# First weights' conversions pinned to the program's order, their low parts on GpSimd, and half of the first batch's sums over v on GpSimd

## The chip, the core and the metric

One core of a Trainium2 chip runs the whole program in one launch. The metric is the device time of an execution in microseconds (us); lower is better. Five engines run side by side, each through its own queue in order: TensorE (PE, its weight loads PEld), VectorE (DVE), ScalarE (ACT), GpSimd (POOL) and SyncE (SP, which here issues every DMA).

## What is computed

Attention with keys and values pooled by 8 along the sequence, for 8 batches of 8 heads, 576 positions and 64 columns a head; then two feed-forward blocks on the 4608 tokens. Cut to what matters:

```
k_p = k.reshape(B, H, 72, 8, 64).mean(axis=3);  v_p likewise
scores = scale * q @ k_p.T;  attn = softmax(scores)
x = (attn @ v_p) as 4608 tokens x 512
h = x @ w_in;  x = maximum(0.01 * h, h) @ w_out          # 512 x 2048, 2048 x 512
xn = x / rms(x) * rms_g
out = (silu(xn @ w_gate) * (xn @ w_val)) @ w_out2
```

## The kernel before

Every fp32 operand of the large products is held as two fp32r tensors, a rounded high part and a low part that is the difference (`split`, line 90: the high part is a cast on ScalarE, L92, the low part a subtraction, L95, on the engine that the caller names). A product then takes three matmuls, high by high, high by low and low by high.

The tokens go through the first feed-forward in nine tiles of 512 (`j` 0 to 8). For each of 16 blocks `f` of 128 hidden columns, `h_unit` (L592) multiplies by the w_in block and makes the two halves of the activation (`ghl`: ScalarE L98 twice, then a VectorE subtraction L605), and `y_unit` (L628), two blocks later, multiplies by the w_out block. In tile 0 the first eight blocks are done for tokens 0 to 255 first, and again for tokens 256 to 511 at the end of the tile (`h0_0_256` and on), because only the first two q tiles of batch 0 are through attention when the tile begins.

The 32 weight blocks (w_i0, w_o0, w_i1, ... w_o15) are read from memory as raw pieces and converted on chip by the class `Weights`, once. A piece is 128 x 512; the last four blocks come as eight pieces of 128 x 256. One piece takes four steps:

- a first pass in place over the upper words on ScalarE (a `prelu`, listed under L98) and one over the lower words on VectorE (TENSOR_SCALAR, L141),
- a join of the two on VectorE (SCALAR_TENSOR_TENSOR, L149),
- the cast to the high part on ScalarE (L92), and
- the subtraction for the low part (L95), on GpSimd and VectorE by turns: w_in blocks on GpSimd and w_out blocks on VectorE; of the halves of a block the first on GpSimd and the second on VectorE.

`step()` ends one piece (join, cast, low part), loads what may be loaded, and begins the next one (the two first passes). Raw pieces lie in slots that later weights take over, the eight half pieces in a ring of three (`raw`) that k and v of the following batches use too.

Attention of batch 0 comes first: `k_prep` and `v_prep` sum eight rows (for batch 0 a VectorE reduction, L239 and L254; for later batches GpSimd adds in halves, `pool_sum`, L229, then L245 or L259), `v_prep` spreads the sum over two heads (`vm`, GpSimd L263, one buffer) and splits it (`vb`). `step_s` is the softmax of one q tile (VectorE L331, L332, L337 to L340 around ScalarE's exponential, L336), `step_x` transposes it and splits it (`at`), `step_av` multiplies by v and leaves the first feed-forward's input (`xhl`).

The order of each engine's queue comes from a scheduler that places an instruction as soon as its own model of time has its operands ready; a conversion whose piece has come in may so stand ahead of attention that was written before it. `keep_in_program_order` pins an instruction behind the one that the program wrote before it on the same engine. From the second half on the order is the written one.

Of the kernel before, what the change touches and what calls it, by code (L numbers as in the profile page):

```python
# [8 lines left out]
F32 = mybir.dt.float32  # L9
# [7 lines left out]
HI, LO = 0, 1  # L17
# [5 lines left out]
def pooled_attention_then_two_ffns(  # L23
# [13 lines left out]
    nc = tc.nc  # L37
# [59 lines left out]
    def prelu(out, in_, alpha, scale=1.0):  # L97
        return nc.scalar.activation(out=out, in_=in_, func=AF.Prelu, scale=scale, alpha=alpha)  # L98
# [8 lines left out]
    class Weights:  # L107
# [5 lines left out]
        def __init__(self, todo, ahead):  # L113
            self.todo = todo
            self.ahead = ahead
            self.loaded = []
            self.begun = []
            self.done = {}
            self.n = 0

        def left(self):
            return bool(self.todo or self.loaded or self.begun)
# [10 lines left out]
        def begin(self):  # L133
            x = self.loaded.pop(0)
            t = x[2]
            top, low = t[:, :, 1], t[:, :, 0]


            prelu(top.bitcast(F32), top.bitcast(F32), 2.0 ** 32, scale=2.0 ** -112)

            nc.vector.tensor_scalar(  # L141
                out=low, in0=low.bitcast(U32), scalar1=0.9374 * 2.0 ** -29, scalar2=None, op0=ALU.mult
            )
            self.begun.append(x)

        def end(self):
            key, at, t, mk = self.begun.pop(0)
            top, low = t[:, :, 1], t[:, :, 0]
            nc.vector.scalar_tensor_tensor(  # L149
                out=top, in0=top, scalar=3, in1=low, op0=ALU.logical_shift_left, op1=ALU.bitwise_or  # L150
            )
            if key not in self.done:
                self.done[key] = mk(f"w_{key[0]}{key[1]}")
            w = self.done[key]
            self.n += 1
            lo_eng = nc.gpsimd if self.n % 2 else nc.vector
            split(nc.scalar, w[:, HI, at], lo_eng, w[:, LO, at], top.bitcast(F32))

        def step(self):
            if self.begun:  # L160
# [87 lines left out]
    def v_prep(b, r):  # L248
        rest = r >= NP
        n = R3 if rest else P  # L250
        x = vraw.pop((b, r))[0:n]
        vs = ap.tile([P, D], F32, tag="vs", bufs=2, name=f"vs{b}_{r}")[0:n]
        if b == 0:
            nc.vector.tensor_reduce(  # L254
                out=vs, in_=x.rearrange("p (r d) -> p d r", r=POOL), axis=AX.X, op=ALU.add
            )
        else:
            pool_sum(x)
            nc.gpsimd.tensor_tensor(out=vs, in0=x[:, 0:D], in1=x[:, D:2 * D], op=ALU.add)  # L259
        m = mask_rest.rearrange("p q h -> p (q h)") if rest else mask_main  # L260
        c = m.shape[1]
        vm = ap.tile([P, 4, D], F32, tag="vm", bufs=1, name=f"vm{b}_{r}")[0:n, 0:c]
        nc.gpsimd.tensor_tensor(  # L263
            out=vm, in0=vs.unsqueeze(1).to_broadcast([n, c, D]),
            in1=m.unsqueeze(2).to_broadcast([n, c, D]), op=ALU.mult,
        )
        if rest:

            t = ap.tile([R3, 4, D], F32R, tag="vbr", bufs=2, name=f"vb{b}_{r}")
            nc.scalar.activation(out=t, in_=vm, func=AF.Copy)  # L270
            z = slice(2 * R1, 3 * R1)
            nc.vector.tensor_tensor(out=t[z], in0=vm[z], in1=t[z].bitcast(F32), op=ALU.subtract)
        else:
            t = ap.tile([P, 2, 2, D], F32R, tag="vb", bufs=4, name=f"vb{b}_{r}")
            split(nc.scalar, t[:, HI], nc.vector, t[:, LO], vm)
        vb[b, r] = t
# [68 lines left out]
    at = {}  # L345
# [234 lines left out]
        W1.load()  # L580
    for x in before:
        run_step(x)
        if x[0] in "sx" and x[2] > 0:
            W1.step()

    gp = {}
# [669 lines left out]
```

## Time and profile before

| | us |
|---|---|
| median of 3 executions | 1825.57 (1824.18 to 1827.65) |
| the profiled execution | 1826.16 |
| its span, first to last instruction | 1824.4 |
| TensorE busy in the span | 1764.8 (97%) |
| VectorE busy | 881.1 (48%) |
| ScalarE busy | 669.4 (37%) |
| GpSimd busy | 557.0 (31%) |

The span is 1.8 us shorter than the execution's time. The shares are means over stages that differ much, so the rows further down are taken by stretch. Start times are counted from the first instruction. In a timeline row the bracket holds the engine's idle time before the instruction and what ended it; neighbours on an engine overlap by some hundredths to a few tenths of a microsecond, so durations add up to somewhat more than the time from start to start. GpSimd's own durations are rough.

### The profile page before, as it was taken

The numbers are of one execution on the slowest core, as the hardware profiler recorded it, in microseconds if no ns is written. First come the engines' busy times: TensorE is split into PE (matmuls) and PEld (weight loads), VectorE is DVE, ScalarE is ACT, GpSimd is POOL, SyncE is SP. The second block draws the span as 40 slices with busy tenths as digits, with TensorE's granted clock in tenths as the row PEclk, the third lists the DMA queues.
The fourth block names the chain that finished last, engine by engine and source line by source line (L and its number), as shares of the span: only waits on it lengthen the run. The fifth ranks groups of instructions, "written<-read, shape, count | busy, mean of one in ns | idle before, by whom it ended". The sixth has DMA issues, their size and how long they took to land.

```text
span 1824.4 us, 23632 instructions
## 1 busy us (share of the span) xinstructions
PE 1764.8 (97%) x8596; PEld 1504.5 (82%) x8596; DVE 881.1 (48%) x1593; ACT 669.4 (37%) x1424; POOL 557.0 (31%) x691
## 2 busy tenths in 40 slices
PE   4899999999999999999999999999999999999999
PEld 3789887888888887888888878989787888988887
DVE  8974445463356555554244336344534533463331
ACT  5754334343343444343433332233232223322220
POOL 2653204243124252111211442244144114513330
PEclk9999999999999999999999999999999999999999
DMA  8832105446365445445442657687676567776562
GB/s 266 292 118 85 47 21 159 151 150 222 104 192 161 157 147 161 144 143 165 159 150 82 230 175 247 188 294 245 237 248 207 187 221 281 247 264 201 197 208 104
DMA packets 175556, 330.81 MB, mean 181 GB/s; under 512 B 54352, under 2 KB 90192, under 8 KB 174928
## 3 DMA queue, kind: packets, MB, share of 16 engines
q1 hardware_dynamic: 175440, 329.31, 54.9%
q8 instruction: 68, 1.11, 0.3%
q14 instruction: 48, 0.39, 0.1%
HBM read 277.87 MB, written 51.38 MB: 180 GB/s over the span
## 4 chain that ended last, share of the span: by engine, by line
PE 87%; DVE 4%; DMA 4%; POOL 2%; issue 1%; ACT 1%; SPq 1%; ACTq 0%; DVEq 0%; POOLq 0%
PE h L592 20%; PE y L628 20%; PE o L1089 14%; PE yv L1014 6%; PE yg L1014 6%; PE xv L1014 4%; PE wv L1014 4%; PE wg L1014 4%; PE xg L1014 4%; PE sc L325 2%; DMA wo<-wo 1%; PE av L395 1%; DMA xst<-y 1%; PE xt L369 1%; PE qt L303 1%
## 5 line engine op out<-in xcount | busy, mean ns | idle before, releaser
L592 PE MATMUL h<-xhl,w_i 128*128 128x512 f32 (+1 forms) x1824 | 438.6, 386 | 3.0 <-ACT xhl L92 1.5
L592 PEld LDWEIGHTS h<-xhl,w_i 128*128 128x128 f32 x1824 | 330.3, 191 | 67.7 <-DVE xhl L95 3.2
L1089 PE MATMUL o<-wo,u 128*128 128x512 f32 x1296 | 315.7, 391 | 5.1 <-DMA wo<-wo 5.1
L1089 PEld LDWEIGHTS o<-wo,u 128*128 128x128 f32 x1296 | 243.0, 188 | 54.1 <-issue 4.3
L628 PE MATMUL y<-ghl,w_o 128*128 128x512 f32 (+1 forms) x1296 | 285.1, 365 | 1.4 <-DVE ghl L605 1.4
L628 PEld LDWEIGHTS y<-ghl,w_o 128*128 128x128 f32 x1296 | 219.0, 191 | 35.1 <-DVE ghl L605 1.8
L605 DVE TENSOR_TENSOR ghl<-g,ghl 128x512 fp32r<-128x512 f32 (+1 forms) x152 | 114.5, 754 | 245.1 <-ACT g L98 241.9
L98 ACT ACTIVATE ghl<-h 128x512 fp32r<-128x512 f32 (+1 forms) x152 | 86.9, 572 | 227.6 <-PE h L592 227.1
L628 PE MATMUL y<-ghl,wr 128*128 128x512 f32 x624 | 158.6, 395 | 0.0
L628 PEld LDWEIGHTS y<-ghl,wr 128*128 128x128 f32 x624 | 115.1, 188 | 22.4
L95 POOL TENSOR_TENSOR u<-e2g,u 128x512 fp32r<-128x512 f32 (+1 forms) x25 | 29.6, 1182 | 287.1 <-ACT u L92 277.7
L229 POOL TENSOR_TENSOR v<-v 128x256 f32<-128x256 f32 (+2 forms) x84 | 61.3, 733 | 111.1 <-DMA v<-in_v_dram 108.5
L1014 PE MATMUL xv<-xa,av 128*128 128x512 f32 (+1 forms) x360 | 85.8, 374 | 6.1 <-ACT e1v L1042 6.1
L98 ACT ACTIVATE g<-h 128x512 f32<-128x512 f32 (+1 forms) x152 | 86.7, 571 | 0.0
L1014 PE MATMUL yv<-T,av 128*128 128x512 f32 (+1 forms) x360 | 85.3, 373 | 0.0
L1014 PE MATMUL yg<-T,ag 128*128 128x512 f32 (+1 forms) x360 | 83.9, 368 | 0.0
L1014 PE MATMUL xg<-xa,ag 128*128 128x512 f32 (+1 forms) x360 | 83.8, 368 | 0.0
L1014 PEld LDWEIGHTS xv<-xa,av 128*128 128x128 f32 x360 | 67.5, 192 | 16.2 <-ACT e1v L1042 6.7
L1014 PEld LDWEIGHTS yv<-T,av 128*128 128x128 f32 x360 | 67.8, 192 | 9.5
L1014 PEld LDWEIGHTS xg<-xa,ag 128*128 128x128 f32 x360 | 66.2, 188 | 9.5
L1014 PEld LDWEIGHTS yg<-T,ag 128*128 128x128 f32 x360 | 66.2, 188 | 9.4
L735 POOL TENSOR_TENSOR parts_g<-raw_g,parts_g 128x256 fp32r<-128x256 f32 (+1 forms) x48 | 33.6, 723 | 100.1 <-ACT parts_g L731 100.1
(166 smaller groups left out, 2594.8 us busy)
## 6 DMA issues: line engine op xcount, KB each, us to landing
wo<-wo SPq DMA_DIRECT2D x120, 512.0 KB
av<-op_v SPq DMA_DIRECT2D x90, 512.0 KB
ag<-op_g SPq DMA_DIRECT2D x90, 512.0 KB
wr<-wo SPq DMA_DIRECT2D x52, 512.0 KB
y<-ye SPq DMA_DIRECT2D x36, 256.0 KB
op_g<-parts_g SPq DMA_DIRECT2D x36, 256.0 KB
op_v<-parts_v SPq DMA_DIRECT2D x36, 256.0 KB
out_dram<-oe SPq DMA_DIRECT2D x36, 256.0 KB
```

Of the source, the lines that this page charges most:

```text
L95: lo_eng.tensor_tensor(out=lo, in0=src, in1=hi.bitcast(F32), op=ALU.subtract)
L98: return nc.scalar.activation(out=out, in_=in_, func=AF.Prelu, scale=scale, alpha=alpha)
L229: nc.gpsimd.tensor_tensor(out=x[:, :n], in0=x[:, :n], in1=x[:, n:2 * n], op=ALU.add)
L303: nc.tensor.transpose(pt[:, c * P:(c + 1) * P], x[:, c * P:(c + 1) * P], ident)
L325: nc.tensor.matmul(pt[:, i * n:(i + 1) * n], y[:, p, :], kblk[b % 2][:, p * n:(p + 1) * n], start=True, stop=True,)
L369: nc.tensor.transpose(pt[:, c * P:(c + 1) * P], e[:, c, 0:P], ident)
L592: nc.tensor.matmul(pt, w[:, sp, c * P:(c + 1) * P], x[:, mp, c, :], start=c == 0 and i == 0, stop=c == n_k - 1 and i == 2,)
L605: nc.vector.tensor_tensor(out=t[:, LO, :], in0=g, in1=t[:, HI, :].bitcast(F32), op=ALU.subtract)
L628: nc.tensor.matmul(pt, w[:, sp, m * P:(m + 1) * P], g[:, mp, a - c0:a - c0 + n], start=ydone[j, a] == 1 and i == 0 and m % per_bank == 0, ...
L735: own(nc.gpsimd.tensor_tensor(out=d[:, :, LO, :], in0=x, in1=d[:, :, HI, :].bitcast(F32), op=ALU.subtract))
L1014: nc.tensor.matmul(pt, wt[:, a, c, sp, :], xt[:, mp, :], start=start and c == 0 and i == 0, stop=c == 1 and i == 2, skip_group_check=not s ...
L1089: nc.tensor.matmul(pt, u[:, sp, m * P:(m + 1) * P], w[:, mp, :], start=f == 0 and i == 0, stop=f == F2 - 1 and i == 2,)
```

## The change

Three edits. The two first passes of every piece are pinned behind what the program wrote ahead of them on their engines, and `step()` is now also called after the second q tile's softmax, after both `step_x` of the first two tiles and after each of the four `av0`, so that it runs seven times and not twice before tile 0 begins. The low parts of all weights are GpSimd's. Of the first batch's six sums over v, numbers 0, 2 and 4 are made by GpSimd as for the later batches.

```diff
--- before.py
+++ after.py
@@ -116,7 +116,6 @@
             self.loaded = []
             self.begun = []
             self.done = {}
-            self.n = 0
 
         def left(self):
             return bool(self.todo or self.loaded or self.begun)
@@ -136,11 +135,14 @@
             top, low = t[:, :, 1], t[:, :, 0]
 
 
-            prelu(top.bitcast(F32), top.bitcast(F32), 2.0 ** 32, scale=2.0 ** -112)
-
-            nc.vector.tensor_scalar(
+            x1 = prelu(top.bitcast(F32), top.bitcast(F32), 2.0 ** 32, scale=2.0 ** -112)
+
+            x2 = nc.vector.tensor_scalar(
                 out=low, in0=low.bitcast(U32), scalar1=0.9374 * 2.0 ** -29, scalar2=None, op0=ALU.mult
             )
+
+            tc.keep_in_program_order(x1)
+            tc.keep_in_program_order(x2)
             self.begun.append(x)
 
         def end(self):
@@ -152,9 +154,7 @@
             if key not in self.done:
                 self.done[key] = mk(f"w_{key[0]}{key[1]}")
             w = self.done[key]
-            self.n += 1
-            lo_eng = nc.gpsimd if self.n % 2 else nc.vector
-            split(nc.scalar, w[:, HI, at], lo_eng, w[:, LO, at], top.bitcast(F32))
+            split(nc.scalar, w[:, HI, at], nc.gpsimd, w[:, LO, at], top.bitcast(F32))
 
         def step(self):
             if self.begun:
@@ -250,7 +250,7 @@
         n = R3 if rest else P
         x = vraw.pop((b, r))[0:n]
         vs = ap.tile([P, D], F32, tag="vs", bufs=2, name=f"vs{b}_{r}")[0:n]
-        if b == 0:
+        if b == 0 and r % 2:
             nc.vector.tensor_reduce(
                 out=vs, in_=x.rearrange("p (r d) -> p d r", r=POOL), axis=AX.X, op=ALU.add
             )
@@ -580,7 +580,7 @@
         W1.load()
     for x in before:
         run_step(x)
-        if x[0] in "sx" and x[2] > 0:
+        if x[0] in ("x", "av0") or x[0] == "s" and x[2] > 0:
             W1.step()
 
     gp = {}
```

The lines move a little: L141 and L149 of before are L140 and L151 of after. The new order at three places follows. First VectorE's queue in the first batch's softmax (ex0_0 and ex0_1 are the exponentials of the first two q tiles, st their maxima and sums, raw_i0 to raw_o1 raw weight pieces, vs sums over v). Before:

```order
L332 TENSOR_TENSOR ex0_1_212<-sc0_1_0_214,st0_1_213 128x288
L337 TENSOR_REDUCE st0_0_196<-ex0_0_195 128x8
L141 TENSOR_SCALAR raw_o0_0_121<-raw_o0_0_121 128x512
L95 TENSOR_TENSOR vb0_2_249<-vm0_2_247,vb0_2_249 128x128
L332 TENSOR_TENSOR ex0_1_212<-sc0_1_1_219,st0_1_213 128x288
L338 TENSOR_SCALAR st0_0_196<-st0_0_196 128x8
L149 SCALAR_TENSOR_TENSOR raw_o0_0_121<-raw_o0_0_121 128x512
L339 RECIPROCAL st0_0_196<-st0_0_196 128x8
L254 TENSOR_REDUCE vs0_5_266<-first12_123 96x64
L141 TENSOR_SCALAR raw_i1_0_128<-raw_i1_0_128 128x512
L337 TENSOR_REDUCE st0_1_213<-ex0_1_212 128x8
L340 TENSOR_TENSOR ex0_0_195<-ex0_0_195,st0_0_196 128x576
```

After:

```order
L332 TENSOR_TENSOR ex0_1_212<-sc0_1_1_219,st0_1_213 128x288
L339 RECIPROCAL st0_0_196<-st0_0_196 128x8
L340 TENSOR_TENSOR ex0_0_195<-ex0_0_195,st0_0_196 128x576
L337 TENSOR_REDUCE st0_1_213<-ex0_1_212 128x8
L95 TENSOR_TENSOR vb0_2_253<-vm0_2_251,vb0_2_253 128x128
L338 TENSOR_SCALAR st0_1_213<-st0_1_213 128x8
L339 RECIPROCAL st0_1_213<-st0_1_213 128x8
L340 TENSOR_TENSOR ex0_1_212<-ex0_1_212,st0_1_213 128x576
L140 TENSOR_SCALAR raw_i0_0_119<-raw_i0_0_119 128x512
L254 TENSOR_REDUCE vs0_5_272<-first12_123 96x64
L95 TENSOR_TENSOR at0_0_279<-xt0_0_284,at0_0_279 128x4x128
L95 TENSOR_TENSOR vb0_3_260<-vm0_3_258,vb0_3_260 128x128
```

The first passes and joins of the first pieces have left the softmax: the first one now follows the second tile's last softmax step, L340.

Second, GpSimd's queue where the weights begin (w_i0, w_o0, ... low parts; vm the spread sums of v; k1 the keys of batch 1). Before:

```order
L263 TENSOR_TENSOR vm0_4_261<-vs0_4_259,mask_rest_65 96x256
L95 TENSOR_TENSOR w_i1_408<-raw_i1_0_128,w_i1_408 128x512
L263 TENSOR_TENSOR vm0_5_268<-vs0_5_266,mask_rest_65 96x256
L95 TENSOR_TENSOR w_i2_466<-raw_i2_0_139,w_i2_466 128x512
L95 TENSOR_TENSOR w_i3_534<-raw_i3_0_143,w_i3_534 128x512
L95 TENSOR_TENSOR w_i9_946<-raw_i9_0_809,w_i9_946 128x512
L229 TENSOR_TENSOR k1_0_872<-k1_0_872 128x256
L95 TENSOR_TENSOR w_i4_610<-raw_i4_0_309,w_i4_610 128x512
L229 TENSOR_TENSOR k1_1_879<-k1_1_879 128x256
L229 TENSOR_TENSOR k1_0_872<-k1_0_872 128x128
L229 TENSOR_TENSOR k1_2_904<-k1_2_904 128x256
```

After:

```order
L263 TENSOR_TENSOR vm0_4_267<-vs0_4_263,mask_rest_65 96x256
L263 TENSOR_TENSOR vm0_5_274<-vs0_5_272,mask_rest_65 96x256
L95 TENSOR_TENSOR w_i0_297<-raw_i0_0_119,w_i0_297 128x512
L95 TENSOR_TENSOR w_o0_320<-raw_o0_0_121,w_o0_320 128x512
L95 TENSOR_TENSOR w_i1_336<-raw_i1_0_128,w_i1_336 128x512
L95 TENSOR_TENSOR w_o1_351<-raw_o1_0_130,w_o1_351 128x512
L95 TENSOR_TENSOR w_i2_366<-raw_i2_0_139,w_i2_366 128x512
L95 TENSOR_TENSOR w_o2_379<-raw_o2_0_141,w_o2_379 128x512
L95 TENSOR_TENSOR w_i3_442<-raw_i3_0_143,w_i3_442 128x512
L229 TENSOR_TENSOR k1_0_918<-k1_0_918 128x256
L229 TENSOR_TENSOR k1_1_925<-k1_1_925 128x256
L229 TENSOR_TENSOR k1_0_918<-k1_0_918 128x128
```

Seven low parts now stand in a row ahead of batch 1's keys, the w_out blocks among them, and none before the last vm.

Third, ScalarE's queue while the first av are made (L98 on a raw piece is its first pass, L92 on a w its cast, xhl the input of the first feed-forward). Before:

```order
L98 ACTIVATE raw_i3_0_143<-raw_i3_0_143 128x512
L376 ACTIVATE atr0_0_274<-xr0_1_300 96x2x128
L92 ACTIVATE w_i2_466<-raw_i2_0_139 128x512
L92 ACTIVATE w_o2_528<-raw_o2_0_141 128x512
L98 ACTIVATE raw_o3_0_145<-raw_o3_0_145 128x512
L98 ACTIVATE raw_i6_0_613<-raw_i6_0_613 128x512
L92 ACTIVATE xhl0_318<-av0_0_0_313 128x256
L92 ACTIVATE w_i3_534<-raw_i3_0_143 128x512
L98 ACTIVATE raw_o6_0_666<-raw_o6_0_666 128x512
L92 ACTIVATE xhl0_318<-av0_0_1_321 128x256
```

After:

```order
L92 ACTIVATE w_o0_320<-raw_o0_0_121 128x512
L98 ACTIVATE raw_i1_0_128<-raw_i1_0_128 128x512
L92 ACTIVATE xhl0_332<-av0_0_0_327 128x256
L92 ACTIVATE w_i1_336<-raw_i1_0_128 128x512
L98 ACTIVATE raw_o1_0_130<-raw_o1_0_130 128x512
L92 ACTIVATE xhl0_332<-av0_0_1_343 128x256
L92 ACTIVATE xhl0_332<-av0_0_2_358 128x256
L92 ACTIVATE w_o1_351<-raw_o1_0_130 128x512
L98 ACTIVATE raw_i2_0_139<-raw_i2_0_139 128x512
L92 ACTIVATE w_i2_366<-raw_i2_0_139 128x512
L98 ACTIVATE raw_o2_0_141<-raw_o2_0_141 128x512
```

A piece's first pass now comes after the cast of the piece before it, where first passes ran ahead by up to five pieces.

SyncE's queue keeps its 797 rows; from the fifth block's loads on, those of weights, k, v and q change places by a few rows.

## Rows read from the trace of the kernel before

**Rows 1.** Page, part 2: busy tenths of TensorE in 40 equal slices.

```profile
PE   4899999999999999999999999999999999999999
```

**Rows 2.** Busy time by stretch; clock, DMA share and GB/s in the last columns.

```profile
0.00:37.20 37.20, 11.95 (x41) 8.49 (x41) 29.78 (x55) 19.26 (x50) 8.93 (x25) 1.00 0.84 257
45.00:113.00 68.00, 61.59 (x419) 55.85 (x419) 67.29 (x126) 49.29 (x121) 42.39 (x52) 0.97 0.68 231
120.00:130.00 10.00, 9.04 (x41) 8.31 (x42) 7.58 (x18) 6.53 (x16) 2.92 (x6) 0.66 0.49 153
140.00:400.00 260.00, 256.24 (x1371) 220.24 (x1370) 122.92 (x272) 99.16 (x254) 73.73 (x134) 0.99 0.34 102
```

The columns are the stretch, its length, then busy time (instructions) of PE, PEld, DVE, ACT and POOL, the granted clock, the DMA share and GB/s.

**Rows 3.** Timeline of TensorE: start, duration, instruction, count, idle before and releaser.

```profile
37.22 1.01 PE L395 MATMUL av<-at,vb 128*128 128x256 f32 x3 [2.50 <-DVE at L95]
...
120.96 1.01 PE L395 MATMUL av<-at,vb 128*128 128x256 f32 x3 [2.58 <-DVE at L95]
...
129.35 0.51 PE L395 MATMUL av<-at,vb 128*128 128x256 f32 x3
...
134.54 0.66 PE L325 MATMUL sc<-kblk,qT 128*128 128x144 f32 x4
...
138.60 0.60 PE L303 MATMUL qt<-ident,q 128*128 128x128 f32 x4
...
140.00 1.68 PE L592 MATMUL h<-xhl,w_i 128*128 128x256 f32 x12
```

**Rows 4.** Timeline of VectorE in the first batch's attention.

```profile
12.70 0.45 DVE L331 TENSOR_REDUCE st<-sc 128x4 f32<-128x288 f32 x1
...
14.07 1.01 DVE L254 TENSOR_REDUCE vs<-first 128x64 f32<-128x512 f32 x1
...
17.52 0.43 DVE L141 TENSOR_SCALAR raw_i<-raw_i 128x512 int32<-128x512 uint32 x1 [1.87 <-DMA raw_i<-in_moe_w_in_dram]
...
36.48 0.69 DVE L95 TENSOR_TENSOR at<-xt,at 128x512 fp32r<-128x512 f32 x1
```

**Rows 5.** Timeline from 45 to 50 us, GpSimd first, then VectorE.

```profile
46.27 1.31 POOL L95 TENSOR_TENSOR w_i<-raw_i,w_i 128x512 fp32r<-128x512 f32 x1 [4.90 <-ACT w_i L92]
...
48.92 1.52 POOL L95 TENSOR_TENSOR w_i<-raw_i,w_i 128x512 fp32r<-128x512 f32 x1 [0.21 <-ACT w_i L92]
...
45.31 0.42 DVE L141 TENSOR_SCALAR raw_i<-raw_i 128x512 int32<-128x512 uint32 x1
45.65 0.68 DVE L149 SCALAR_TENSOR_TENSOR raw_o<-raw_o 128x512 int32<-128x512 int32 x1
...
46.59 1.53 DVE L149 SCALAR_TENSOR_TENSOR raw_i<-raw_i 128x512 int32<-128x512 int32 x1
...
49.42 1.31 DVE L605 TENSOR_TENSOR ghl<-g,ghl 128x256 fp32r<-128x256 f32 x1 [0.15 <-ACT g L98]
```

**Rows 6.** Timeline, single instructions of VectorE and GpSimd.

```profile
61.00 0.41 DVE L605 TENSOR_TENSOR ghl<-g,ghl 128x256 fp32r<-128x256 f32 x1
...
124.22 0.74 POOL L95 TENSOR_TENSOR w_i<-raw_i,w_i 128x256 fp32r<-128x256 f32 x1 [2.90 <-ACT w_i L92]
...
63.62 0.74 POOL L229 TENSOR_TENSOR k<-k 128x256 f32<-128x256 f32 x1 [0.77 <-DMA k<-in_k_dram]
...
55.47 0.45 POOL L229 TENSOR_TENSOR k<-k 128x128 f32<-128x128 f32 x1
...
57.15 0.31 POOL L245 TENSOR_TENSOR kp<-k 128x64 f32<-128x64 f32 x1
```

**Rows 7.** Groups by line and form, 45.0 to 112.9 us: busy, mean ns, idle before.

```profile
L149 DVE SCALAR_TENSOR_TENSOR raw_o<-raw_o 128x512 int32<-128x512 int32 x9 | 8.5, 947 | 0.1
L95 DVE TENSOR_TENSOR w_o<-raw_o,w_o 128x512 fp32r<-128x512 f32 x10 | 7.7, 771 | 0.0
...
L95 POOL TENSOR_TENSOR w_i<-raw_i,w_i 128x512 fp32r<-128x512 f32 x10 | 13.9, 1394 | 23.5 <-ACT w_i L92 23.5
```

**Rows 8.** Timeline of VectorE, one wait for a raw half piece.

```profile
118.59 0.84 DVE L141 TENSOR_SCALAR raw_o<-raw_o 128x256 int32<-128x256 uint32 x1 [4.96 <-POOL v L229]
```

## The prediction, made before the changed kernel was run

> **What bounds the kernel now.** I read the slices of the page first. TensorE is busy in nine tenths or more of every slice but the first, which holds 46 us [rows 1]; from 140 to 400 us it is busy for 256.24 of 260 us at a granted clock of 0.99 [rows 2]. Work that is moved among the other engines can therefore gain only ahead of 140 us, and what is gained there is carried to the end if the order after it is the same, as it is from the second half on and nearly so from tile 2. Next come the stretches. Until 37.2 us TensorE works for 11.95 us and VectorE for 29.78 [rows 2]: the program begins with a chain over VectorE. The first product with v starts at 37.22, released by VectorE's `at`, which ended at 37.17 [rows 3, 4]. From 45 to 113 us VectorE is busy for 67.29 of 68 us and GpSimd for 42.39 [rows 2].
>
> That last pair is not what it seems. A join takes 0.68 us at 45.65, and 1.53 at 46.59, where it ends half a microsecond behind the low part that GpSimd began at 46.27. A subtraction that takes 0.41 at 61.00 takes 1.31 at 49.42 beside the low part of 48.92 [rows 5, 6]. So VectorE's busy time there holds waits for GpSimd, and a low part costs VectorE nearly as much as if it ran there.
>
> The Trainium skill, page "SBUF — State Buffer", section "Who interferes with whom", says the same more sharply: an instruction of VectorE with two SBUF inputs, or in a two-port mode, and one of GpSimd that reads SBUF shut each other out for their whole length, and a reduction on VectorE does not take part. It speaks against this change twice, since subtractions go where they hold the shared port longer, and three reductions that leave it alone become adds that hold it. The rows at 46.59 and 49.42 agree. Without the lock VectorE would be freed by what it gives away (the rival with the whole head start, below); with it, the sum of the next paragraphs holds.
>
> **A check of that account.** Say that in-place passes, joins, low parts, `ghl` and `ex` products on VectorE and everything on GpSimd take one shared turn. From 45.0 to 112.9 us VectorE has 18 joins and 10 low parts at 0.68, 16 first passes at 0.42, 8 `ghl` at 0.41 and 4 at 0.68, and some 8.6 us of smaller ones: 40.4 us. GpSimd has 10 low parts at 1.31 and 2 halves at 0.74, batch 1's keys (5 times 0.74 + 0.45 + 2 x 0.31, so 9.1), and 9.7 of v (1.9 a sum, with 0.4 for vm): 33.4 [rows 5 to 7]. Together 73.8 us of durations in 67.9 us; neighbours overlap a little, which gives 1.08 us of durations for each us of time. The turn is full throughout. A change that adds to the turn loses there what it adds, divided by 1.08.
>
> **Part 1, the softmax ahead of the conversions.** Ahead of the second tile's `at` (36.48, rows 4) VectorE loses three sums (3 x 1.02), five first passes (2.1), five joins (3.4), two low parts (1.4) and one vb part (0.4), so 10.4 us, and the wait of 1.87 for the first raw piece, which by then will have come [rows 4, 5]. That alone would put `at` at 24.2. But the softmax can't begin before the first scores at 12.70 [rows 4], 13.5 us of VectorE's work stand between, which gives 26.2, and the six vm through one buffer go back and forth between three engines. I take 28 (bounds 26 and 30): a head start of 9.2 us for the first product.
>
> **Part 2, half of the sums on GpSimd.** Three times 0.74 + 0.45 + 0.31 = 4.5 us [rows 6]. GpSimd is busy for 8.93 of the first 37.2 us, so they are hidden; if the vm chain behind them were late it would cost up to those 4.5. I take nothing.
>
> **Part 3, the low parts.** Fourteen whole and four half ones leave VectorE (about 11.2 us) and cost GpSimd 14 x 1.31 + 4 x 0.74 = 21.3: 10.1 us more of the shared turn. And the pinned order puts each piece's first pass behind the cast of the piece before, so nothing is converted ahead.
>
> **The sum.** When the first low part starts, about 28 us, these are left for the turn. GpSimd: 28 x 1.31, 8 x 0.74, keys 9.1, five v of 1.9: 61.2. VectorE: 26 first passes, 27 joins, eight halves of each at six tenths, 8 `ghl` at 0.41 and 7 at 0.68, and 6.6 of small ones: 49.2. That is 110.4, over 1.08 102.2, and I add 1.5 for holes where a row of low parts has nothing beside it: the last piece is done at 131.7. The second half of w_i15 is two half pieces earlier (2 x 1.4 / 1.08 = 2.6), at 129.1. From there TensorE has 6 of the 12 matmuls of h_15 and 15 of y_13 before `h0_0_256`, 27 units of 256 columns at some 0.14 us (12 in 1.68) [rows 3], 3.6 us with overlap off: 132.7, where the kernel before has 140.00. But that one had by then done two av, two scores, a qt and a kt that the new order puts later (0.51 and 0.66 twice each and 0.60, rows 3: 2.9 by duration, of which I take 2.4 since neighbours overlap), and the second pair's `av` now waits for the last v of batch 1, behind the last low parts on GpSimd, for which I take 1.0. The gain is 140.0 - 132.7 - 2.4 - 1.0 = **3.9 us**.
>
> The head start of 9.2 us is thus mostly given back, since the stretch to the last conversion goes from TensorE's pace to that of the shared turn. What was late before also goes: at 118.59 VectorE had waited 4.96 us for a half piece with `at` queued behind it, and TensorE 2.58 for that `at` [rows 3, 8]; from 120 to 130 us the granted clock was 0.66, a mixture of 1.2 and 2.4 GHz behind that gap [rows 2]. This is in the 140.0.
>
> SyncE's queue: as many loads; those of the last half pieces wait for three buffers that v shares, and each waits for a low part on GpSimd, now the slowest engine of the chain. The stores of w_o0 to w_o7 in the same queue wait for GpSimd too. I take nothing for it, since the turn and not the loads was full before, and 4.96 us as the price of one late piece.
>
> The span would go from 1824.4 to 1820.5. The profiled execution was 1826.16, 0.6 above the median of 1825.57, so against the median I forecast 1821.7.
>
> **Rivals.**
>
> *The head start is kept whole.* If TensorE, not the turn, paces the new order (low parts of GpSimd falling beside VectorE work that reads PSUM: scores, maxima, `at`, `xhl`), 9.2 us stay: 1816.4. For it: 42.39 us of GpSimd in 68 leave room. Against: the turn was full in the same stretch.
>
> *No change.* The pinned steps overlap less than the free order did, 1.04 in place of 1.08: 106.2 us, the last piece at 135.7 with the holes, `h0_0_256` at 136.7, a gain of 140 - 136.7 - 3.4 = -0.1: 1825.7. For it: up to five first passes ran ahead before, none do now.
>
> *Slower: the chain through one piece.* Join (0.68), cast (about 0.7), low part (1.31) and the next join behind it: 2.7 us a piece, which uses the turn only part of the time, while keys, v and `ghl` come in lumps that hide little. Then durations pass one by one: 28 + 110.4 = 138.4, `h0_0_256` at 139.4, -2.8 us, and with one late half piece reaching TensorE as before (2.58 us) 5.4: 1831.0. The average step, counting a half as 0.6, may be 3.28 us before anything is lost; my sum has it at 3.16 and this case at 3.37. So a tenth of a microsecond a step decides.
>
> *The scheduler undoes it*, so that the new order is not the one meant: the rows of the order ahead rule that out, the softmax does come first.
>
> **How the numbers follow.** The forecast (a gain of 2 to 7 us) has 0.48, the whole head start 0.15, no change 0.20, slower 0.17. A measurement tells 0.2% from no change, 3.65 us. Of the forecast's 0.48, 0.33 lie beyond that; with the 0.15 of the head start faster has 0.48. Within 0.2% are 0.15 of the forecast, 0.20, and 0.01 of the slower case: 0.36. Slower has 0.16. The range leaves out the far end of the head start (0.06) and of the slower case (0.10): 1815.5 to 1829.5.
>
> **What would show it.** Right: the first av near 28 us; low parts on GpSimd in a row some 2.7 to 3.3 us apart; the last near 132; VectorE's joins and first passes often at 1.2 us or more; `h0_0_256` near 133. Wrong: first av after 31 (the vm chain), or the last low part before 126 (no full turn) or after 137 (the chain), or a clock below full over a long part of 60 to 130 us, since TensorE waiting for each low part could fall to the lower level; then its products would take twice as long, and that is in no term above.

## The result: ten microseconds slower, lost behind the conversions

| | before | after |
|---|---|---|
| median, us | 1825.57 | 1835.72 |
| lowest to highest | 1822.30 to 1831.46 | 1829.85 to 1840.99 |
| profiled execution | 1826.16 | 1840.99 |
| span of it | 1824.4 | 1839.3 |

The ratio is 1.0052, with a 95% interval of 1.0034 to 1.0070: slower by 6 to 13 us, outside the range of the prediction. The profiled execution of after is its slowest, so its trace shows more of the loss (14.9 us in the span) than the median (10.2).

The views of the profile of after in the order in which before was read. First the busy time by stretch (columns as in [rows 2]):

```profile
0.00:37.20 37.20, 16.83 (x62) 12.95 (x62) 26.84 (x49) 16.88 (x48) 14.00 (x34) 1.00 0.81 245
45.00:113.00 68.00, 59.97 (x371) 53.62 (x372) 62.59 (x105) 47.08 (x114) 50.77 (x54) 0.92 0.67 223
113.00:130.00 17.00, 17.00 (x118) 15.75 (x117) 11.12 (x22) 9.19 (x23) 8.44 (x11) 1.00 0.37 105
130.00:150.00 20.00, 13.36 (x88) 12.70 (x88) 7.83 (x16) 6.48 (x18) 12.78 (x25) 0.88 0.33 90
150.00:200.00 50.00, 46.04 (x314) 43.19 (x313) 27.73 (x58) 19.97 (x63) 20.91 (x42) 0.91 0.35 98
140.00:400.00 260.00, 249.59 (x1317) 214.49 (x1316) 123.74 (x266) 96.74 (x247) 77.95 (x147) 0.97 0.33 98
```

The same of before, for the stretches that [rows 2] lacks:

```profile
113.00:130.00 17.00, 14.42 (x76) 13.00 (x75) 9.51 (x21) 7.71 (x19) 5.51 (x10) 0.80 0.43 130
130.00:150.00 20.00, 20.00 (x159) 19.48 (x159) 10.31 (x20) 7.12 (x24) 13.14 (x26) 1.00 0.34 101
150.00:200.00 50.00, 49.98 (x330) 45.55 (x329) 24.41 (x55) 21.33 (x58) 20.02 (x38) 1.00 0.31 85
```

Until 37.2 us TensorE is busy for 4.9 us more than before. From 45 to 113 us it gives that back: 371 of its matmuls (of differing widths) fall in that stretch, 419 in before [rows 2]. From 113 to 130 it is ahead again, 17.00 us busy at full clock against 14.42 at 0.80. Then it turns. From 130 to 200 us it is idle for 10.6 us (70 less 13.36 and 46.04) where before had none, at a lower clock. The forecast had it that nothing behind 140 us would change.

TensorE's timeline shows the place (as in [rows 3]):

```profile
29.01 1.01 PE L395 MATMUL av<-at,vb 128*128 128x256 f32 x3 [1.40 <-DVE at L95]
...
125.59 0.87 PE L395 MATMUL av<-at,vb 128*128 128x256 f32 x6
...
133.13 0.51 PE L400 MATMUL av<-atr,vb 96*128 96x256 f32 x2 [2.78 <-DVE vb L272]
...
136.64 0.52 PE L592 MATMUL h<-xhl,w_i 128*128 128x256 f32 x3
...
145.79 0.80 PE L400 MATMUL av<-atr,vb 96*128 96x256 f32 x2 [3.86 <-DVE vb L272]
...
182.81 1.08 PE L369 MATMUL xt<-ident,ex 128*128 128x128 f32 x4 [3.42 <-DVE ex L340]
```

The first product with v came at 29.01, as forecast, and `h0_0_256` at 136.64. But the `av` of batch 1 now stop in the middle: `L400` multiplies by `vb1_4` and `vb1_5`, the last two v pieces, and waits 2.78 and 3.86 us for them. The third wait, at 182.81, is at the border to tile 1, where the attention that came late behind those products has nothing left to hide under. At the end of each of the last two waits the granted clock falls to 0.50 for 6.8 us, that is 1.2 in place of 2.4 GHz. By an estimate some 3.1 us are lost apiece, half of the 6.11 and 6.18 us in which TensorE is busy there:

```profile
145.10:151.90 6.80, 6.11 (x28) 6.11 (x29) 2.13 (x5) 1.97 (x7) 5.58 (x13) 0.50 0.43 122
182.70:189.50 6.80, 6.18 (x20) 5.29 (x21) 2.43 (x8) 2.60 (x10) 1.44 (x4) 0.50 0.13 29
```

What the v pieces waited for stands in the queues. SyncE's, before and then after (L214 loads `v1_4` and `v1_5`; L130 and L129 load weights):

```profile
90.14 2.01 SPq L214 DMA_DIRECT2D v<-in_v_dram  x3
...
110.13 1.99 SPq L214 DMA_DIRECT2D v<-in_v_dram  x3
```

```profile
122.23 2.02 SPq L214 DMA_DIRECT2D v<-in_v_dram  x3
124.35 0.38 SPq L129 DMA_DIRECT2D raw_i<-in_moe_w_in_dram  x1
125.38 6.40 SPq L129 DMA_DIRECT2D raw_o<-in_moe_w_out_dram  x2
133.79 1.99 SPq L214 DMA_DIRECT2D v<-in_v_dram  x3
```

and GpSimd's of after:

```profile
115.41 1.51 POOL L95 TENSOR_TENSOR w_o<-raw_o,w_o 128x512 fp32r<-128x512 f32 x1
...
124.60 0.76 POOL L95 TENSOR_TENSOR w_i<-raw_i,w_i 128x256 fp32r<-128x256 f32 x1 [0.82 <-ACT w_i L92]
129.43 1.27 POOL L229 TENSOR_TENSOR v<-v 96x256 f32<-96x256 f32 x2 [4.07 <-DMA v<-in_v_dram]
...
133.02 0.74 POOL L95 TENSOR_TENSOR w_i<-raw_i,w_i 128x256 fp32r<-128x256 f32 x1 [0.85 <-ACT w_i L92]
...
136.17 0.74 POOL L95 TENSOR_TENSOR w_o<-raw_o,w_o 128x256 fp32r<-128x256 f32 x1 [0.82 <-ACT w_o L92]
140.89 1.26 POOL L229 TENSOR_TENSOR v<-v 96x256 f32<-96x256 f32 x2 [3.97 <-DMA v<-in_v_dram]
```

The half pieces wait for their loads too. VectorE's first pass of the second half of w_i15 in after, whose load is the one at 124.35:

```profile
130.09 0.29 DVE L140 TENSOR_SCALAR raw_i<-raw_i 128x256 int32<-128x256 uint32 x1 [4.98 <-DMA raw_i<-in_moe_w_in_dram]
```

A load follows a release: the low part at 133.02 ends at 133.76, and the load of `v1_5` is issued at 133.79. The three slots of the ring are given out in the order in which the program asks for them. Seven steps in place of two ahead of tile 0 mean that the half pieces ask earlier, and v no earlier. The order of SyncE's queue (five rows of before that follow each other, then six of after) says it:

```
L214 DMA v1_4_1280<-in_v_dram 32x1x512 x3
L130 DMA raw_o13_0_1211<-in_moe_w_out_dram 128x1024
L130 DMA raw_i14_0_1321<-in_moe_w_in_dram 128x2x256
L130 DMA raw_i14_256_1329<-in_moe_w_in_dram 128x2x256
L130 DMA raw_o14_0_1337<-in_moe_w_out_dram 128x512
```

```
L129 DMA raw_i15_0_1268<-in_moe_w_in_dram 128x2x256
L214 DMA v1_4_1325<-in_v_dram 32x1x512 x3
L129 DMA raw_i15_256_1365<-in_moe_w_in_dram 128x2x256
L129 DMA raw_o15_0_1373<-in_moe_w_out_dram 128x512
L129 DMA raw_o15_256_1380<-in_moe_w_out_dram 128x512
L214 DMA v1_5_1384<-in_v_dram 32x1x512 x3
```

`v1_4` stood ahead of all eight half pieces and now stands behind five; `v1_5` stood behind three and now stands behind all.

### The profile page after: what moved, and what is told of

Its sections match the earlier page's. It is cut to its first block, busy times and chain, and to the rows that moved or that the text cites. A ratio compares the mean times of both kernels' runs of the same rounds, so it can differ in the third digit from the quotient of the medians.

```text
span 1839.3 us, 23655 instructions
## 1 busy us (share of the span) xinstructions
PE 1773.1 (96%) x8596; PEld 1509.5 (82%) x8596; DVE 884.2 (48%) x1572; ACT 668.3 (36%) x1424; POOL 583.4 (32%) x718
## 4 chain that ended last, share of the span: by engine, by line
PE 82%; DVE 5%; DMA 5%; POOL 3%; ACT 2%; issue 2%; SPq 1%; POOLq 0%; ACTq 0%; DVEq 0%
PE h L592 18%; PE y L628 18%; PE o L1089 14%; PE yv L1014 6%; PE yg L1014 6%; PE xv L1014 4%; PE wv L1014 4%; PE wg L1014 4%; PE xg L1014 4%; PE sc L325 2%; DMA k<-in_k_dram 1%; DMA xst<-y 1%; DMA wo<-wo 1%; PE av L395 1%; PE xt L369 1%
## 5 line engine op out<-in xcount | busy, mean ns | idle before, releaser
L592 PE MATMUL h<-xhl,w_i 128*128 128x512 f32 (+1 forms) x1824 | 446.2, 389 | 3.9 <-ACT xhl L92 2.4
L592 PEld LDWEIGHTS h<-xhl,w_i 128*128 128x128 f32 x1824 | 334.2, 194 | 67.3 <-ACT xhl L92 3.1
L98 ACT ACTIVATE ghl<-h 128x512 fp32r<-128x512 f32 (+1 forms) x152 | 87.0, 572 | 204.8 <-PE h L592 204.3
L98 ACT ACTIVATE g<-h 128x512 f32<-128x512 f32 (+1 forms) x152 | 86.8, 571 | 0.0
```

What stands on the lines that cost most here:

```text
L592: nc.tensor.matmul(pt, w[:, sp, c * P:(c + 1) * P], x[:, mp, c, :], start=c == 0 and i == 0, stop=c == n_k - 1 and i == 2,)
```

## Experiments: where the ten microseconds went

All times are medians. The ratio is to the kernel before as it ran beside that experiment (1823.4 to 1825.4), with its 95% interval; two experiments are compared by their medians. The letters are names of theories, which each expectation states with its range.

**A buffer of their own** for `v1_4` and `v1_5`, in the changed kernel (e1) and in the kernel before (e2):

```diff
-        t = ap.tile([P, 512], F32, tag="raw", bufs=3, name=f"v{b}_{r}") if tile_ is None else tile_
+        own = b == 1 and r >= NP
+        t = tile_
+        if t is None:
+            t = ap.tile([P, 512], F32, tag="vown" if own else "raw", bufs=1 if own else 3, name=f"v{b}_{r}")
```

> The changed kernel, with one more buffer of 128x512 in which v1_4 and v1_5 (the last two v pieces of batch 1) land, in place of the ring of three that they share with the half pieces of the last weights. Theory R (the ring): in the trace of after the time is not lost where the conversions run but behind them; v1_4 and v1_5 are loaded at 122.2 and 133.8 us (90.1 and 110.1 before), since the five extra steps put the half pieces ahead of them in the ring, and TensorE waits for them 2.78 us at 133.1, 3.86 at 145.8, and by the attention that is late behind them 3.42 at 182.8, with half clock for 6.8 us behind each of the last two. R expects all three waits under 0.6 us, 10.1 us less waiting and 6.8 less of half clock: some 17 us under after, 1817 to 1824, so faster than before. Theory G (GpSimd's added 10.1 us of low parts in a full shared turn are the loss): no change against after, 1832 to 1839. Theory C (short waits for conversions ahead of 113 us let the clock fall): the 10.2 us of half clock at 46, 70 and 108 us stay and only part comes back, 1827 to 1832.

> The kernel before with the same extra buffer for v1_4 and v1_5. It tells what of e1 is owed to the buffer itself. R: v1_4 and v1_5 were not late there, but v1_4 held a slot for which a half piece waited (VectorE 4.96 us at 118.6, TensorE 2.58 at 121.0, half clock from 120.4 to 127.2): up to 2.6 + 3.4 less, 1819 to 1825. G and C: nothing, 1824 to 1828.

e1 took 1826.45 us, ratio 1.0009 (0.9999 to 1.0018): 9.3 us under after. No `av` waits for v any more (the products of batch 1 by TensorE's timeline, line numbers moved by three), nor anything at the border:

```profile
125.48 0.51 PE L398 MATMUL av<-at,vb 128*128 128x256 f32 x3
125.83 0.28 PE L403 MATMUL av<-atr,vb 96*128 96x256 f32 x1
...
134.14 0.62 PE L398 MATMUL av<-at,vb 128*128 128x256 f32 x3 [1.72 <-DVE xhl L95]
134.60 0.28 PE L403 MATMUL av<-atr,vb 96*128 96x256 f32 x1
```

So theory R has the cause, but not the size: 17 us were expected from the profiled waits and 9.3 came, and nothing is left over as a gain. By the time alone e1 lies between the ranges of R and of C, short waits ahead of 113 us that let the clock fall. The stretches show which it is (before, after and e1):

```profile
0.00:140.00 140.00, 104.74 (x635) 93.31 (x636) 120.08 (x226) 85.10 (x207) 67.62 (x104) 0.96 0.69 220
140.00:200.00 60.00, 59.98 (x414) 55.55 (x413) 28.96 (x64) 25.38 (x74) 24.74 (x48) 1.00 0.32 91
```

```profile
0.00:140.00 140.00, 107.39 (x641) 94.84 (x642) 112.60 (x194) 82.19 (x202) 81.30 (x107) 0.96 0.67 212
140.00:200.00 60.00, 52.18 (x348) 49.12 (x347) 29.68 (x62) 22.24 (x70) 29.51 (x60) 0.89 0.34 96
```

```profile
0.00:140.00 140.00, 102.65 (x637) 89.88 (x637) 114.93 (x198) 83.19 (x205) 87.74 (x120) 0.91 0.68 216
140.00:200.00 60.00, 59.83 (x412) 55.10 (x411) 32.04 (x71) 26.84 (x76) 29.73 (x59) 1.00 0.33 95
```

By 140 us the three have begun about as many products: 635, 641 and 637. So after isn't behind there, neither by C nor by the first wait for v, of 2.78 us, which was counted in the 17 all the same (e1 waits elsewhere by then, 1.72 us at 134.14). From 140 to 200 us after begins 348 where the others begin 414 and 412: the loss lies there, at the last two waits and the clock behind them. Besides, the 17 were read from after's slowest execution; the two traces are 15.6 us apart (spans of 1839.3 and 1823.7).

e2 took 1827.41, 1.0016 (1.0004 to 1.0028), where R allowed a gain; the buffer isn't what helps e1, since by itself it costs 2.

**The step condition**, alone on the kernel before (e3), and undone in the changed kernel (e4):

```diff
-        if x[0] in "sx" and x[2] > 0:
+        if x[0] in ("x", "av0") or x[0] == "s" and x[2] > 0:
```

> The kernel before with only the new condition for calling step(): seven calls and not two ahead of tile 0; low parts by turns, sums on VectorE, nothing pinned. R: the ring's order is now that of after (v1_4 behind the first half of w_i15, v1_5 last), with none of the other edits, so TensorE waits for v1_4 and v1_5 as in after, 2.5 to 4 us each, and the time is 8 to 17 us over before: 1834 to 1843. G: low parts are by turns, so 1824 to 1828.

> The changed kernel with the old condition for step(): pinned first passes, all low parts on GpSimd, half of the sums on GpSimd, but two steps ahead of tile 0 as before, so v1_4 and v1_5 stand ahead of the half pieces again. R: no wait over 1 us for v1_4 or v1_5, no half clock behind; but the pinned conversions now begin later and TensorE may wait for weights in tile 0 by some us: 1820 to 1832. G: as slow as after or slower, with the low parts the bound, 1834 to 1842.

e4: 1826.72, 1.0008 (0.9996 to 1.0019), 9.0 us under after, by another road than e1. e3: 1827.59, 1.0016 (1.0005 to 1.0028), where R had 1834 to 1843. The late order alone costs 2 us: in e3 `v1_4` and `v1_5` are loaded at 113.50 and 124.28, 9 us ahead of after, and TensorE, without the head start, doesn't wait for `v1_5`. So the order does its full harm only together with the other edits of the change.

**The low parts**, by turns in the changed kernel (e5; the edit, less the line that sets `self.n` to 0), by turns with the old step condition (e6), and all on GpSimd in the kernel before (e7):

```diff
-            split(nc.scalar, w[:, HI, at], nc.gpsimd, w[:, LO, at], top.bitcast(F32))
+            self.n += 1
+            lo_eng = nc.gpsimd if self.n % 2 else nc.vector
+            split(nc.scalar, w[:, HI, at], lo_eng, w[:, LO, at], top.bitcast(F32))
```

> The changed kernel with the low parts by turns on GpSimd and VectorE as before; the pinned first passes, the seven steps ahead of tile 0 (so v1_4 and v1_5 behind the half pieces in the ring) and the half sums stay. The extra steps alone had given no wait over 0.5 us for v1_4 or v1_5, with these loaded at 113.5 and 124.3 us. Theory R2 (the late place in the ring costs only together with a ring that turns slowly, since all low parts queue on GpSimd): v1_5 is loaded ahead of 128 us, the waits for v1_4 and v1_5 are under 1.5 us together (6.6 in after), 1822 to 1828. Rival O (the place in the ring is enough where the head start has been won): the two waits stay at 2 to 4 us each, 1831 to 1837.

> The changed kernel with the old condition for step() and the low parts by turns: pinned first passes and half of the sums on GpSimd are what is left of the change. Against the changed kernel with the old condition alone (1826.7) only the low parts move back. Theory T (what the ring does not explain of the missing gain went into the shared turn of VectorE and GpSimd, 10.1 us more of it by the low parts): 3 to 6 us less, 1820 to 1824, and faster than before. Rival N (a low part costs the chain about the same on either engine): 1825 to 1828.

> The kernel before with only the low parts of all weights on GpSimd. The ring keeps the order of before (v1_4 ahead of all half pieces). T: 10.1 us more of a turn that is full from 45 to 113 us, over 1.08: the last conversion up to 9 us later, of which TensorE sees 3 to 9: 1828 to 1835. N, or a turn that is not full: 1824 to 1827.

e5: 1837.65, 1.0068 (1.0049 to 1.0087), as slow as after. R2 fails in the time, though the waits for v all but vanish (0.68 us); O had nearly the time, 1831 to 1837, but by waits of 2 to 4 us for v that are not there. By 140 us e5 has begun 670 products, more than any kernel above, and from there to 200 us only 314. What came instead is at the border (TensorE, then SyncE's queue and ScalarE, of e5):

```profile
176.78 2.29 PE L328 MATMUL sc<-kblk,qT 128*128 128x144 f32 x8 [8.08 <-DVE at L95]
```

```profile
158.38 10.03 SPq L217 DMA_DIRECT2D v<-in_v_dram  x6
168.46 0.41 SPq L647 DMA_DIRECT2D y<-ye  x1
```

```profile
174.92 0.59 ACT L644 COPY ye<-y 128x512 f32<-128x512 f32 x1 [8.87 <-DMA y<-ye]
175.40 0.60 ACT L92 ACTIVATE at<-xt 128x512 fp32r<-128x512 f32 x1
```

The loads of batch 2's last v pieces, late themselves and waiting for the ring, hold SyncE's queue for 10.03 us; the store of y stands behind them, ScalarE's next copy of y behind the store, the cast of `at` behind the copy, and TensorE waits 8.08 us. That v's place in the ring is behind this wait too is shown by e9 below, where a buffer of their own for `v1_4` and `v1_5` takes it away.

e6: 1827.01, 1.0006 (0.9993 to 1.0019); T had 1820 to 1824, so here rival N was right: against e4 (1826.72), a low part costs about the same on either engine. e7: 1830.25, 1.0034 (1.0021 to 1.0047): in the old order, without the head start, all low parts on GpSimd cost 5.1 us, as T had it.

**The pinning alone** (e8: the two `keep_in_program_order` of the change on the kernel before):

> The kernel before with only the two first passes pinned (old condition for step(), low parts by turns, all six sums on VectorE): the softmax of the first two tiles stands ahead of the conversions by this alone. Expected of the head start: first product with v at 29 to 32 us (three sums of 1.02 us each more on VectorE than in after). T: the turn gets nothing more than before, so the head start is kept in part, 2 to 5 us: 1820 to 1823.5. N: given back behind the conversions, 1824 to 1827.

1828.93, 1.0023 (1.0009 to 1.0036): the first product with v came at 32.08 us, 5.1 earlier than before, and the time was 3.8 longer. Neither theory had it as high.

**Both mended** (e9: e5 with the buffer of e1), and **a ring of four** (`tag="raw", bufs=4`) in e4 (e10), in before (e11) and in after (e12):

> The changed kernel with the low parts by turns and with one buffer of their own for v1_4 and v1_5. With the low parts by turns alone (1837.65) TensorE was furthest ahead in tile 0 of all kernels until 160 us (613 products of the first feed-forward started, 572 in before), and then waited 8.08, 1.09 and 2.12 us at the border to tile 1 for batch 1's attention, whose third q tile had its scores at 146.6 us (134.5 in before), with half clock from 171.0 to 191.5. Theory R3 (the late place of v1_4 and v1_5 delays batch 1's attention, and what was won in tile 0 is paid at the border): scores of the third q tile before 138 us, no wait over 1.5 us at the border, about 11 us of waits and 8 of half clock less: 1817 to 1822, faster than before. Rival B (the border's wait comes from the stores of y in SyncE's queue and the low parts by turns, not from v): it stays over 4 us, 1829 to 1838.

> The changed kernel with the old condition for step() and a ring of four buffers in place of three. With the old condition alone (1826.7) v1_4 and v1_5 are in time, the last whole low part comes at 114.1 us, but the eight half pieces take until 139.0. Theory H (the half pieces are paced by their loads through the ring, about 5 us to land and three slots, and that is what ate the rest of the forecast gain): last low part before 134 us, 1820 to 1824. Rival T (the shared turn and other waits ahead of 114 us ate it): last low part little earlier or not seen by TensorE, 1825 to 1828.

> The kernel before with a ring of four buffers. H: its half pieces too are paced by the ring (the low parts of the first halves stand at 108.8, 111.5, 124.2 and 127.1 us), and TensorE's wait of 2.58 us at 121.0 with half clock behind it goes: 1819 to 1823. T: the same as before within 2 us, 1824 to 1828.

> The changed kernel with a ring of four buffers and nothing else: v1_4 and v1_5 stay behind the half pieces in the order of the loads, but each load can go one release earlier. R3 (the order is what costs): the loads come some 3 us earlier, so part of the 10 us comes back, 1828 to 1833. H (the number of slots): nearly all of it, 1822 to 1827.

e9: 1824.37, 0.9996 (0.9984 to 1.0008). The buffer that cost 2 us on before gives 13.3 on e5, and the waits at the border are gone: R3's mechanism holds, though the gain over before that it had with it does not come. The ring of four only lost: e10 1835.20 (1.0050, 1.0038 to 1.0062), e11 1827.94 (1.0011, 1.0001 to 1.0020), e12 1842.83 (1.0089, 1.0072 to 1.0106). Theory H falls, and for e12 R3 was wrong as well, which had expected 1828 to 1833: a fourth slot does not make up for the late order, and with the old order it costs time. In e10 ScalarE's copy of y waits 6.12 us for a store at the border, as in e5. Why one more slot brings that on stays open.

## Experiments: why nothing is left of the head start

With the ring mended, e1, e4, e6 and e9 stand within 2 us of before. e9 shows best where the head start goes (before for 0 to 45 us, then e9):

```profile
0.00:45.00 45.00, 18.73 (x71) 14.98 (x72) 37.51 (x70) 25.04 (x61) 11.30 (x26) 1.00 0.88 267
```

```profile
0.00:45.00 45.00, 25.19 (x130) 21.33 (x131) 33.93 (x65) 24.06 (x64) 14.72 (x35) 0.77 0.86 260
45.00:113.00 68.00, 55.10 (x352) 48.09 (x350) 62.29 (x114) 44.19 (x106) 39.54 (x53) 0.95 0.72 238
```

By 45 us TensorE has begun 130 products in e9 and 71 in before, 59 more. From 45 to 113 it begins 352 where before began 419 [rows 2], 67 fewer. The head start is given back, and a little more. The busy times (6.46 us more, then 6.49 less) point the same way, but they are no measure of work here, because the clocks differ: e9's is shown at 0.77 up to 45 us. The 1.00 of before up to 45 us is doubtful: three products of an `av` take 1.01 us at 37.22, as long as at 120.96, and 0.51 at 129.35 [rows 3].

**All low parts on VectorE** (`lo_eng = nc.vector`), in e9 (e13) and in before (e14):

> The changed kernel with one buffer of its own for v1_4 and v1_5 and with all low parts of the weights on VectorE. With that buffer and the low parts by turns (1824.37) no wait of the tail is left, TensorE is 6.5 us ahead of before at 45 us (19.8 us idle, 26.3 in before), and at 113 us nothing of it is left: in between it waits for casts and low parts of w_i blocks. Theory T (the turn of VectorE and GpSimd paces the conversions from 45 to 113 us, whoever starts them): on VectorE a low part takes 0.68 us and not 1.31, and holds the turn only so long, so 14 whole and 4 half ones cost some 10 us less of the turn: 1816 to 1821, faster than before. Rival L (the loads of the raw pieces pace them, or one engine's own queue: VectorE was busy for 62 of 68 us): no gain, 1823 to 1828.

> The kernel before with all low parts of the weights on VectorE, nothing else. All of them on GpSimd had given 1830.25, by turns 1825. T: the third step of the same ladder, some 10 us less of the turn: 1818 to 1823. L: VectorE's own queue grows by 14 x 0.68 + 4 x 0.41, 11 us, in a stretch in which it is busy for 67 of 68 us: 1827 to 1834.

e13: 1828.48, 1.0026 (1.0014 to 1.0039); e14: 1831.78, 1.0041 (1.0026 to 1.0057). By the account of the turn, 10 us had been taken off it, and the time went up. In e14 the first product with v moved to 41.37 us, so part of its loss is ahead of the stretch; e13 has it at 27.32 and is the cleaner one. The shared turn isn't the pace by itself. Rival L, VectorE's own queue or the loads, has e14 in its range (1827 to 1834) and e13 just above it.

**Without the joins** (`scalar_tensor_tensor` in `end()` left out, so that the weights are never put together from their two words), in before (e15) and in e9 (e16):

> The kernel before without the join of the first weights' pieces (28 whole and 8 half ones; the low words are left out of the weights, so that conversions cost less): from 45 to 113 us VectorE loses 18 joins of 0.68 us or more. It is the base for the next run. Theory P (the conversions pace TensorE from 45 to 113 us, whichever engine of the chain is the slowest): some gain, 2 to 6 us, 1818 to 1823. Rival Q (TensorE or the loads pace that stretch): 1823 to 1827.

> The changed kernel with the low parts by turns and a buffer of its own for v1_4 and v1_5 (1824.37, level with before), also without the joins of the first weights' pieces. P: the head start of 6.5 us at 45 us was lost to the pace of the conversions; with these lighter it is kept, so that this kernel is 4 to 7 us under the kernel before without joins, 1813 to 1818. Q: the two stay level within 2 us, since what took the head start away is something else (loads, or attention work that is only put later).

e15: 1818.24, 0.9967 (0.9955 to 0.9979). e16: 1812.86, 0.9933 (0.9919 to 0.9948), 5.4 us under e15 where e9 is level with before. By stretch, e16:

```profile
0.00:45.00 45.00, 25.07 (x132) 21.65 (x133) 32.23 (x64) 25.51 (x66) 16.12 (x36) 1.00 0.87 261
45.00:113.00 68.00, 63.76 (x438) 58.03 (x437) 55.06 (x105) 52.33 (x126) 38.65 (x53) 1.00 0.74 255
```

From 45 to 113 us TensorE is idle for 4.2 us, where it was for 12.9 in e9, with about as many products begun at 45 us (132 and 130). So the work of the conversions paces that stretch (P). The other values in the weights don't account for it: from the last stores of tile 2 to the end of the span e15 and e16 take 1440.0 and 1443.6 us, before 1440.2. Whether a join counts as a link of its piece's chain, or as load on VectorE, in whose queue the attention stands too, this doesn't separate. One caution: in e15 the first product with v is at 33.60 us, 3.6 earlier than in before, since joins had stood in the softmax too; and in e16 it is at 31.56, 3.4 later than in e9; so e15 against e16 doesn't have the full head start between them, and e9 against e16 is the firmer pair.

**The step turned round**, so that it begins the next piece before it ends the last, in e9 (e17) and e1 (e18):

```diff
+            n = len(self.begun)
+            if self.loaded:
+                self.begin()
-            if self.begun:
+            if n:
                 self.end()
             while self.todo and len(self.loaded) < self.ahead(self.todo[0]):
                 self.load()
-            if self.loaded:
-                self.begin()
```

> The changed kernel with the low parts by turns, a buffer of its own for v1_4 and v1_5, and step() turned round: it begins the next piece (both first passes) before it ends the last one. In the changed kernel's trace the pieces of the first weights follow each other at 2.66 us: join 1.3 beside the low part of the piece before, cast 0.7, low part 1.3, with the first passes between. Theory P (that chain through one piece paces TensorE from 45 to 113 us): with the first passes a piece ahead no join waits for ScalarE, some 0.3 us a piece: 1818 to 1823, faster than before. Rival S (the shared port and VectorE's total work pace it, not the order within a step): 1823 to 1827.

> The same turned step() with all low parts on GpSimd, so the changed kernel with the buffer for v1_4 and v1_5 and the new step. Against 1826.45 without the turned step: P: 1820 to 1824. S: 1825 to 1829.

e17: 1824.72, 1.0003 (0.9992 to 1.0014). e18: 1824.95, 0.9999 (0.9989 to 1.0009). No gain: rival S in e17, and e18 a hair under its range. In the trace of e17, its fastest execution, 506 products are begun by 113 us where e9 has 480, but by 200 us 1059 against 1056: what the turned step wins in the stretch is gone again behind it. So the order within a step is not what cost the gain. That leaves the work of the conversions as a whole, VectorE's and GpSimd's together, which e16 bears out and nothing here shows apart from VectorE's other work; which engine's share is the binding one is not settled, since neither all low parts on GpSimd nor all on VectorE was better than by turns. No version with the whole computation beat the kernel before by more than its interval.

## Why the prediction was wrong, step by step

The forecast of 1821.7 was missed by 14.0 us. Some 9 of them are the late v pieces, by e1 and e4. The rest is the gain of 3.9 that did not come, and about one more.

- *The softmax ahead of the conversions*: first av at 28 (26 to 30), measured 29.01. Right, and with it the half sums at no cost: with them in e6 the first av is at 28.52, without them in e8 at 32.08, about what the three sums of 1.02 us [rows 4] come to.
- *Low parts and the turn*: 2.7 to 3.3 us apart was right (28.88, 31.52, 34.61 at the start, where a join beside a low part takes 1.33 us, 1.53 in [rows 5]). In the sum the eight half pieces took 10.4 us (2.6 for two) and the whole ones were done at 131.7 less that, 121.3. Measured, the whole ones were done at 116.9, sooner, and the halves took from there to 136.9, because they waited for loads through the ring. So `h0_0_256` began 3.4 us earlier than in before and not 7.3. The trace of before showed such gaps (of its halves on GpSimd one stands at 111.54 and the next at 124.22, of which [rows 6] has the second), and the sum priced them by the turn all the same.
- *SyncE's queue*: "I take nothing". **This is the step that failed.** It names the right resource, the three buffers that v shares, and looks only at what the half pieces wait for, not at who waits behind the half pieces. *The second pair's `av`*, for which 1.0 was taken, waited 2.78 and 3.86 us, and 3.42 more at the border, with 6.8 us of half clock at two of them. e1 and e4 give back 9.3 and 9.0 us of the 10.2.
- *A gain ahead of 140 us is carried to the end*: only while the attention of the next batch keeps its distance. What is late in tile 0 is paid at the border to tile 1, at 182.8 us here and at 176.8 in e5.
- *The gain of 3.9*: not there in e1, e4 or e9. The turn of 1.08 us of durations a microsecond gave a last conversion and thereby a gain; TensorE's own balance by stretch (130 and 352 products in e9 against 71 and 419) says that the head start is gone by 113 us, and e16 that the conversions take it. e13 shows why the account was no measure of pace: it calls 10 us of turn a gain, and none came. The Trainium skill, page "SBUF — State Buffer", section "Who interferes with whom", was right on what it says, that the two lock each other out for the length of an instruction: in after a join from 35.13 beside the low part from 34.61 takes 1.33 us and not 0.68. The error was mine, to add locked lengths up into a time for the stretch.
- *The rivals*: the slower one had the sign and not the mechanism. Its chain of 2.7 us a piece is there (2.66), but e17 and e18 turn its order round and gain nothing, and its late half piece was to cost 2.58 us once. *The clock*, named as being in no term, was 0.92 from 45 to 113 us against 0.97 [rows 2].

## What to carry to other kernels

Where a pool's slots are given out in program order, a call that is moved earlier pushes every later user of that pool back: list who asks for the slots, in order, before and after, and ask who waits for the ones that fell behind. Price the last pieces of a stage by their own limit (here the loads), not by the rate of the stage. A head start that ends in a stretch paced by something else is no gain; compare what TensorE gets through in that stretch, in instructions and not in busy time where the clock differs, before counting it.

## What was not expected of the hardware

The same edit had opposite signs by its surroundings: one buffer of 128x512 cost 2.2 us on before and gave 9.3 and 13.3 on after and e5. A wait of TensorE may cost more than its length: with those of 3.86 and 3.42 us the granted clock fell to 0.50 for 6.8 us each. The length alone doesn't tell: in after the wait of 2.78 us ahead of 133.13 shows no such fall, while in before the shorter one of 2.58 ahead of 120.96 [rows 3] does, at 120.4, before it has ended.
